# Seven block products in place of eight for w_out, and a written order of rounds, in a float32 FFT and MLP kernel

## The chip, the cores and the metric

The kernel runs on one core of one Trainium2 chip. The metric is the device time of one execution in microseconds. A core has engines that run side by side, each with its own queue of instructions: TensorE (PE; weight loads are shown apart as PEld), VectorE (DVE), ScalarE (ACT), GpSimd (POOL, not used here) and SyncE (SP), which issues the DMAs here. They wait for each other by semaphores. Matmuls write to PSUM (eight banks), from which ACT and DVE read.

## The reference

`x` is (8, 3008, 256) in float32; `w_in` is (256, 2048), `w_out` (2048, 256).

```python
X = np.fft.rfft(x, axis=1)
Xr, Xi = (X.real.astype(np.float32), X.imag.astype(np.float32))
Yr = Xr @ w_r - Xi @ w_i + b_r
Yi = Xr @ w_i + Xi @ w_r + b_i
lam = 0.01
Yr = np.sign(Yr) * np.maximum(np.abs(Yr) - lam, 0.0)
Yi = np.sign(Yi) * np.maximum(np.abs(Yi) - lam, 0.0)
Y = Yr.astype(np.float64) + 1j * Yi.astype(np.float64)
y = np.fft.irfft(Y, n=x.shape[1], axis=1)
...
h = np.maximum(x @ w_in, 0.0)
return (h * h @ w_out).astype(np.float32)
```

The second part takes `y`, as 24064 rows of 256.

## The kernel before

A transform of 3008 = 47 * 64 points is done as one of 47 and one of 64. Per batch: stage A (`fft_a`, 13 groups: load `xin`, fold to `f`, matmuls to `psa`, copy to `eva`, store to DRAM scratch), then for each of 12 pairs of residues (`fft_b`) stage B (load `bin`, matmuls to `psb`, copy to `x`), the mix with w_r and w_i (`psm1`, `psm2`, then bias and threshold in `e`, `t`, `z`) and stage C (`psc`, `evc`, store to a second scratch); at last stage D (`inverse`: load `din`, matmuls to `psd`, unfold to `dx`), which gives the columns `xt` of tokens for the two products with w_in and w_out.

Those two run over 52 chunks of columns: 48 of 470 tokens and 4 of 376. For each chunk and each of 16 blocks f of 128 hidden units, `moe_mm1` makes `ph` (L179 to L181), ReLU on ACT (L484) and a square on DVE (L485) give `g`, and `moe_mm2` adds the product with w_out to two PSUM accumulators `po`, one for each half of the 256 outputs. `moe_out` copies them out (L499) after the last f.

A float32 operand is split exactly into a high and a low part of 12 bits: `split` makes `gh` from `g` by a copy on ACT (L173) and `gl` by a subtraction on DVE (L174). `mm3` then uses three passes, high-high, high-low, low-high (L179, L180, L181), in a format called float32r. Some small products (B, D, and all of the first batch) take float32 operands whole; the trace then shows two instructions for one matmul.

The order is partly written and partly made by a scheduler. The main loop runs over chunks and f; `pend` and `LAG = 2` put the w_out product of an f two places behind its w_in product, and `active` is a list of generators (the transform of the next batch, stage D of the next chunk) from which each step takes as much as is due by a count of PE cycles. A tile framework then sets the final order on each engine by its own priorities, and places waits where a buffer or a value is not ready. Buffers come from pools: four PSUM banks for the transform (`ps_f`), two for `ph`, two for `po`. Ahead of the main loop stands the first batch with the weights: `load_win` and `load_wout` load pieces in turn, `narrow` makes float32 of 64-bit words (L217 to L222), and `split` cuts them.

Of the kernel before, what the change touches and what calls it, by code (L numbers as in the profile page):

```python
# [48 lines left out]
# Upper words of 2^-127 and of float32's largest value as float64, read as float32.  # L49
# [4 lines left out]
def groups_of(b):  # L54
    """The small group comes last in an even batch and first in an odd one, so that two meet."""
    return GROUPS if b % 2 == 0 else GROUPS[-1:] + GROUPS[:-1]


def token_order(b):
    """Position in the sequence of each column: by group of n2, n1 = 0..23, then n1 = 46..24."""  # L60
    n1 = np.r_[np.arange(NR), N1 - np.arange(1, NR)]
    return np.concatenate([((64 * n1[:, None] + 47 * (g + np.arange(w))) % S).reshape(-1) for g, w in groups_of(b)])


def folded_rows():
    """Positions in the sequence that are added and subtracted, by group: n1 and 47 - n1; -1 for none."""
# [10 lines left out]
def _cs(num, den):  # L77
    """cos and sin of 2 pi num / den, exact at the multiples of a quarter turn."""
# [8 lines left out]
def tables():  # L87
    """Transform matrices; they depend on the shapes alone."""
# [41 lines left out]

@with_exitstack
def fft_mix_moe(ctx: ExitStack, tc: tile.TileContext, xp, w_r, w_i, b_r, b_i,
# [5 lines left out]
    sb = ctx.enter_context(tc.tile_pool(name="sb", bufs=2))  # L138
    dr = ctx.enter_context(tc.tile_pool(name="dr", bufs=2, space=bass.MemoryType.DRAM))
    ps_f = ctx.enter_context(tc.tile_pool(name="ps_f", bufs=4, space=bass.MemoryType.PSUM))  # L140
    ps_h = ctx.enter_context(tc.tile_pool(name="ps_h", bufs=2, space=bass.MemoryType.PSUM))
    ps_o = ctx.enter_context(tc.tile_pool(name="ps_o", bufs=1, space=bass.MemoryType.PSUM))
# [14 lines left out]
    wmf = [sb.tile([P, 3, D], F32, tag="xh", name=f"wmf{k}", bufs=2) for k in range(2)]  # L157
# [4 lines left out]
    def ldt(name):  # L162
        return sb.tile([P, 512], F32, tag="ld", name=name, bufs=8)

    def evt(name):
        return sb.tile([P, 512], F32, tag="ev", name=name, bufs=4)

    def pst(name):
        return ps_f.tile([P, 512], F32, tag="f", name=name)

    def split(src, hi, lo):
        """src = hi + lo, exactly."""
# [3 lines left out]
    def mm3(out, lt, rt, start, stop):  # L176
# [79 lines left out]
    def rolling(pieces, depth):  # L256
        """Runs the pieces one per step, their loads `depth` steps ahead."""
        q = []
        for p in pieces:
            next(p)  # L260
            q.append(p)
            if len(q) > depth:
                for _ in q.pop(0):
                    pass
# [363 lines left out]
```

## Time and profile before

| | |
|---|---|
| median of 3 runs | 2694.76 us (2693.82 to 2699.69) |
| profiled execution, first to last instruction | 2694.1 us |
| mean granted TensorE clock | 0.996 |
| matmul records | 14088 |
| VectorE busy | 1841.4 us |
| ScalarE busy | 1434.1 us |
| first `ph` matmul begins at | 123.67 us |
| data moved by DMA | 163.44 MB |

In the profile a line of a group has the line of the program, engine, operation, output <- input, shape, count, then the busy time in us and the mean of one in ns, then the engine's idle time just ahead of them with what ended it. The chain of waits is followed back from the last instruction; each of its pieces has a start, a length, both in us, and its engine and line. A line of the stretches has the bounds in us, the length, the busy time and count of PE, PEld, DVE, ACT and POOL, then the granted clock, the share of the DMA engines and GB/s.

### The profile page before, as it was taken

To read this page: it belongs to the slowest core of one execution; us is meant where nothing else is said; L and a number is where in the kernel's file an instruction comes from. 1 tells how busy PE (TensorE), PEld (TensorE's weight loads), DVE (VectorE), ACT (ScalarE), POOL (GpSimd) and SP (SyncE) were. 2 spreads that over 40 slices of the span, in tenths; PEclk is the share of its full clock that TensorE was granted. 3 is DMA by queue.
4 is the path that set the end of the run, shared out by engine and by line. 5 is a ranking of instruction groups with operands and counts; after the bars stand their busy time and mean duration, and the time that the engine had idled before them with its cause. 6 is when DMAs were issued, how large, how long until landed. Compare 5 with 4: busy or idle time off the path is not lost.

```text
span 2694.1 us, 37380 instructions
## 1 busy us (share of the span) xinstructions
PE 2655.6 (99%) x14088; PEld 2387.3 (89%) x14088; DVE 1841.4 (68%) x3375; ACT 1434.1 (53%) x2649; POOL 0.2 (0%) x4
## 2 busy tenths in 40 slices
PE   6899999999999999999999999999999999999999
PEld 5689989989899898998989989899899989899888
DVE  5877766767667777667676776666767677655555
ACT  5755555545555555555555554555555555444444
POOL 0000000000000000000000000000000000000000
PEclk8999999999999999999999999999999999999999
DMA  8621122111221113211032110321103211100000
GB/s 239 203 69 50 45 87 75 45 40 35 79 89 43 45 34 97 75 39 49 27 97 70 46 52 21 107 68 42 49 20 107 70 43 34 47 31 21 8 15 15
DMA packets 113240, 163.44 MB, mean 61 GB/s; under 512 B 9267, under 2 KB 72995, under 8 KB 113059
## 3 DMA queue, kind: packets, MB, share of 16 engines
q1 hardware_dynamic: 113059, 161.05, 19.3%
q8 instruction: 111, 1.82, 0.3%
q14 instruction: 70, 0.57, 0.1%
HBM read 86.04 MB, written 74.97 MB: 60 GB/s over the span
## 4 chain that ended last, share of the span: by engine, by line
PE 95%; DMA 2%; DVE 1%; ACT 1%; issue 0%; SPq 0%; ACTq 0%; DVEq 0%
PE po L179 13%; PE ph L179 13%; PE po L180 13%; PE ph L180 13%; PE po L181 13%; PE ph L181 13%; PE psd L464 3%; PE psb L351 3%; PE psm L181 2%; PE psm L179 2%; PE psm L180 2%; PE psc L180 1%; PE psc L179 1%; PE psa L179 1%; PE psa L180 1%; PE psa L181 1%
## 5 line engine op out<-in xcount | busy, mean ns | idle before, releaser
L484 ACT ACTIVATE g<-ph 128x470 f32<-128x470 f32 (+1 forms) x832 | 463.0, 557 | 636.1 <-PE ph L181 633.1
L485 DVE TENSOR_TENSOR g<-g 128x470 f32<-128x470 f32 (+1 forms) x832 | 532.2, 640 | 355.1 <-ACT g L484 351.8
L174 DVE TENSOR_TENSOR gl<-g,gh 128x470 fp32r<-128x470 f32 (+1 forms) x832 | 532.2, 640 | 310.7 <-ACT gh L173 300.3
L173 ACT CAST gh<-g 128x470 fp32r<-128x470 f32 (+1 forms) x832 | 483.6, 581 | 416.4 <-DVE g L485 411.6
L179 PE MATMUL po<-gh,wo 128*128 128x470 f32 (+1 forms) x1664 | 644.7, 388 | 0.6
L179 PE MATMUL ph<-xt,wi 128*128 128x470 f32 (+1 forms) x1664 | 622.1, 374 | 1.2 <-ACT xt L173 1.2
L180 PE MATMUL po<-gl,wo 128*128 128x470 f32 (+1 forms) x1664 | 621.5, 374 | 0.0
L180 PE MATMUL ph<-xt,wi 128*128 128x470 f32 (+1 forms) x1664 | 620.4, 373 | 0.0
L181 PE MATMUL po<-gh,wo 128*128 128x470 f32 (+1 forms) x1664 | 619.9, 373 | 0.0
L181 PE MATMUL ph<-xt,wi 128*128 128x470 f32 (+1 forms) x1664 | 617.5, 371 | 0.0
L179 PEld LDWEIGHTS ph<-xt,wi 128*128 128x128 f32 x1664 | 314.3, 189 | 39.4 <-ACT xt L173 1.6
L181 PEld LDWEIGHTS po<-gh,wo 128*128 128x128 f32 x1664 | 314.0, 189 | 38.9
L180 PEld LDWEIGHTS ph<-xt,wi 128*128 128x128 f32 x1664 | 315.8, 190 | 36.4
L181 PEld LDWEIGHTS ph<-xt,wi 128*128 128x128 f32 x1664 | 313.1, 188 | 38.4
L179 PEld LDWEIGHTS po<-gh,wo 128*128 128x128 f32 x1664 | 314.7, 189 | 30.0 <-DVE o L499 2.9
L180 PEld LDWEIGHTS po<-gl,wo 128*128 128x128 f32 x1664 | 315.0, 189 | 26.1 <-DVE gl L174 0.6
L398 DVE TENSOR_TENSOR z<-e,t 64x256 f32<-64x256 f32 x336 | 140.9, 419 | 8.1
L179 PE MATMUL psm<-wm,xh 128*128 128x256 f32 x504 | 143.6, 285 | 0.0
L181 PE MATMUL psm<-wm,xl 128*128 128x256 f32 x504 | 142.3, 282 | 0.0
L180 PE MATMUL psm<-wm,xh 128*128 128x256 f32 x504 | 142.1, 282 | 0.0
L464 PE MATMUL psd<-tD,din 120*128 120x120 f32 (+1 forms) x832 | 126.4, 275 | 5.6 <-DMA din<-s 5.6
L351 PEld LDWEIGHTS psb<-tB,bin 128*128 128x128 f32 x768 | 109.4, 194 | 24.0 <-ACT tMs L173 13.6
(75 smaller groups left out, 2317.0 us busy)
## 6 DMA issues: line engine op xcount, KB each, us to landing
bin<-s SPq DMA_DIRECT2D x96, 256.0 KB
s<-evc SPq DMA_DIRECT2D x96, 256.0 KB
s<-eva SPq DMA_DIRECT2D x96, 240.0 KB
din<-s SPq DMA_DIRECT2D x96, 240.0 KB
outT_dram<-o SPq DMA_DIRECT2D x96, 235.0 KB
xin<-in_xp_dram SPq DMA_DIRECT2D x84, 240.0 KB
w<-in_moe_w_in_dram SPq DMA_DIRECT2D x8, 512.0 KB
w<-in_moe_w_out_dram SPq DMA_DIRECT2D x8, 512.0 KB
```

Of the source, the lines that this page charges most:

```text
L173: nc.scalar.copy(hi, src)
L174: nc.vector.tensor_sub(lo, src, hi.bitcast(F32))
L179: nc.tensor.matmul(out, l0, r0, start=start, stop=False)
L180: nc.tensor.matmul(out, l0, r1, start=False, stop=False)
L181: nc.tensor.matmul(out, l1, r0, start=False, stop=stop)
L351: nc.tensor.matmul(ps[:, k, :, q, :], tv[:, q, k], tB[:, 0:r + 2:r + 1], start=True, stop=True)
L398: nc.vector.tensor_sub(z[64 * c:64 * c + 64, q], e[src, c], t[src, c])
L464: nc.tensor.matmul(ps[:, k, part], t[:, s:s + P], tD[:n, tab + part, :n], start=True, stop=True)
L484: nc.scalar.activation(g[:, :n], ph[:, :n], AF.Relu)
L485: nc.vector.tensor_mul(g[:, :n], g[:, :n], g[:, :n])
```

## The change

It does three things.

**Seven products for eight.** Two blocks f, the two halves of the 256 outputs and two halves of a chunk's columns make a 2 x 2 by 2 x 2 block product, which is done with seven block products and some sums (a form of Strassen's scheme). The sums on the weights are made once, into `w7`, seven blocks of 128 x 128 for each pair of f, before the main part. The sums on the hidden values (`sums`) are made per pair on DVE, in `g`, now seven blocks of half the columns (236, with two columns shared by the halves; 188 in the short chunks). `split` is done on all seven at once (1652 columns). The square moves to ACT. The products stay in four PSUM banks (`PLACES`) and are put together after the last pair (`put_together`).

**Rounds written by hand.** The main part stands in `manual_schedule`, where the written order is each engine's order. A round r has the w_in product of pair r, the w_out product of pair r - 2, and at named places (`load`, a1, p1, v1, p2, a2, v2) the steps of the transform: `plan_a` (one group a round), `plan_b` (one pair of residues in three rounds), `plan_d` (two in a chunk of eight rounds). Stage B of a batch begins 51 rounds after that of the one before; A takes 13 of the rounds between.

**Buffers and the start.** The transform has two PSUM banks in place of four, `ph` has one buffer of two banks, `po` four banks. Everything of the first batch, all weights, and stage A of the second batch stand in `start`, in pools of their own, ahead of the rounds.

```diff
+PLACES = ((0, 0, 0), (2, 0, 1), (6, 1, 0), (5, 1, 1), (4, 2, 0), (3, 2, 1), (1, 3, 0))
+NPR = 7
+NU = NF // 2
+PAIR = 3
+TURN = 15
...
+                    def use(h, j=j):
+                        a = h.rearrange("p (f e m) -> p f e m", f=2, e=2)
+                        w7 = tl("w7", (P, NPR, P), bufs=1)
+                        nc.scalar.copy(w7[:, 0:3:2], a[:, :, 0])
+                        nc.scalar.copy(w7[:, 1], a[:, 1, 1])
+                        nc.vector.tensor_add(w7[:, 4], a[:, 0, 1], a[:, 1, 1])
+                        nc.vector.tensor_sub(w7[:, 6], w7[:, 4], a[:, 0, 0])
+                        nc.vector.tensor_sub(w7[:, 5], a[:, 0, 0], a[:, 0, 1])
+                        nc.vector.tensor_sub(w7[:, 3], a[:, 1, 0], w7[:, 6])
+                        split(w7, wo_[0][:, j], wo_[1][:, j])
...
+                r = r0 + i
+                at(r - 2, "load", load)
+                at(r, "v1", folded)
+                at(r, "a2", high)
+                at(r, "v2", low)
+                at(r + 1, "p1", points)
+                at(r + 1, "a2", out)
...
+                r = r0 + PAIR * i
+                at(r - 1 if i == 0 else r - 2, "load", load)
+                at(r, "p2", points)
+                at(r + 1, "a1", take)
...
+                at(r + 2, "p1", mix)
+                at(r + 2, "v2", biased)
+                at(r + 3, "v1", threshold)
+                at(r + 3, "a2", turned)
...
-        nc.scalar.activation(g[:, :n], ph[:, :n], AF.Relu)
-        nc.vector.tensor_mul(g[:, :n], g[:, :n], g[:, :n])
-        split(g[:, :n], gh[:, :n], gl[:, :n])
-        return gh, gl
+    def squares(c, ph):
+        m, t0 = halves(cols[c])
+        g = opnd("g", F32)
+        for t in range(2):
+            nc.scalar.activation(g[:, t:4:2, :m], ph[:, :, t * t0:t * t0 + m], AF.Relu)
+        nc.scalar.activation(g[:, 0:4, :m], g[:, 0:4, :m], AF.Square)
+        return g
+    def sums(c, g):
+        m, _ = halves(cols[c])
+        nc.vector.tensor_sub(g[:, 4:6, :m], g[:, 1:4:2, :m], g[:, 0:2, :m])
+        nc.vector.tensor_sub(g[:, 6, :m], g[:, 3, :m], g[:, 4, :m])
+        nc.vector.tensor_sub(g[:, 1, :m], g[:, 6, :m], g[:, 2, :m])
-    def moe_mm2(po, gg, n, f):
-        for k in range(2):
-            es = slice(k * P, k * P + P)
-            mm3(po[k][:, :n], (wo_[0][:, f, es], wo_[1][:, f, es]),
-                (gg[0][:, :n], gg[1][:, :n]), f == 0, f == NF - 1)
+    def mm2(c, j, po, gg):
+        m, _ = halves(cols[c])
+        for s, bank, half in PLACES:
+            mm3(po[bank][:, half * m:half * m + m], (wo_[0][:, j, s], wo_[1][:, j, s]),
+                (gg[0][:, s, :m], gg[1][:, s, :m]), j == 0 and half == 0, j == NU - 1,
+                skip_group_check=True)
...
+        nc.scalar.copy(p1, p[0])
+        add, sub = nc.vector.tensor_add, nc.vector.tensor_sub
+        add(o[0][:, 0], p[2], p1)
+        add(o[0][:, 1], p[6], p1)
+        add(o[1][:, 0], p[5], o[0][:, 1])
...
+    with tc.manual_schedule():
+        for r in range(last + LAG):
+            c, j = divmod(r, NU)
+            run(r, "load")
+            k = r - 1
+            if k in hid:
+                m, _ = halves(cols[k // NU])
+                gg[k] = opnd("gh", F32R), opnd("gl", F32R)
+                nc.scalar.copy(gg[k][0][:, :, :m], hid[k][:, :, :m])
+            run(r, "a1")
+            if r < last:
+                ph = mm1(c, j)
+            run(r, "p1")
+            if r < last:
+                g = squares(c, ph)
+            if k in hid:
+                nc.vector.tensor_sub(gg[k][1][:, :, :m], hid.pop(k)[:, :, :m],
+                                     gg[k][0][:, :, :m].bitcast(F32))
+            run(r, "v1")
+            if r < last:
+                sums(c, g)
+                hid[r] = g
+            k = r - LAG
+            if k >= 0:
...
+                mm2(cc, jj, pos[cc], gg.pop(k))
+            run(r, "p2")
+            run(r, "a2")
+            if k >= 0 and jj == NU - 1:
+                put_together(cc, pos.pop(cc))
+            run(r, "v2")
```

On PE, in the middle of the program, this stood for one f before (numbers in names tell buffers apart; two accumulators `po`):

```order
L179 MATMUL psm_12776<-wm_85,xh 128x256
L180 MATMUL psm_12776<-wm_86,xh 128x256
L181 MATMUL psm_12776<-wm_85,xl 128x256
L179 MATMUL po_12571<-gh,wo_909 128x470
L180 MATMUL po_12571<-gl,wo_909 128x470
L181 MATMUL po_12571<-gh,wo_910 128x470
L179 MATMUL po_12572<-gh,wo_909 128x470
L180 MATMUL po_12572<-gl,wo_909 128x470
L181 MATMUL po_12572<-gh,wo_910 128x470
```

After, the same lines of `mm3` are L186 to L188. This is the beginning of the w_out part of a round, with a product of stage C ahead of it:

```order
L186 MATMUL psc<-zh,tMs 128x512
L187 MATMUL psc<-zl,tMs 128x512
L188 MATMUL psc<-zh,tMs 128x512
L186 MATMUL po_12206<-gh,wo_529 128x236
L187 MATMUL po_12206<-gl,wo_529 128x236
L188 MATMUL po_12206<-gh,wo_530 128x236
L186 MATMUL po_12206<-gh,wo_529 128x236
L187 MATMUL po_12206<-gl,wo_529 128x236
L188 MATMUL po_12206<-gh,wo_530 128x236
L186 MATMUL po_12207<-gh,wo_529 128x236
```

Six matmuls of 470 columns for one f became 21 of 236 for two, in one stretch, and the transform's products stand at fixed places between the w_in and the w_out part.

On DVE, before, in the main part the square and the low part alternate for each f, with the transform's steps between them:

```order
L485 TENSOR_TENSOR g<-g 128x470
L357 TENSOR_TENSOR x<-x 128x256
L174 TENSOR_TENSOR gl<-g,gh 128x470
L174 TENSOR_TENSOR xl<-x,xh 128x768
L485 TENSOR_TENSOR g<-g 128x470
L174 TENSOR_TENSOR gl<-g,gh 128x470
L380 TENSOR_TENSOR e<-psm_11922,bias_82 128x512
```

After, two rounds of it (L801 is the low part of seven blocks, L750 to L752 are `sums`):

```order
L801 TENSOR_TENSOR gl<-g,gh 128x1652
L231 TENSOR_TENSOR x<-x 128x256
L697 TENSOR_TENSOR xt_9255<-dx,xt_9254 128x2x235
L750 TENSOR_TENSOR g<-g 128x472
L751 TENSOR_TENSOR g<-g 128x236
L752 TENSOR_TENSOR g<-g 128x236
L606 TENSOR_TENSOR xl<-x,xh 128x768
L801 TENSOR_TENSOR gl<-g,gh 128x1652
L639 TENSOR_TENSOR zl<-z,zh 128x512
L750 TENSOR_TENSOR g<-g 128x472
```

The low part of a round's pair stands between its sums and those of the next round, and every step of the transform (v1 ahead of the sums, v2 behind) has a fixed place in that cycle.

On DVE, around the begin of the main part, before: `wo` splits stand on both sides of the first squares (L485).

```order
L174 TENSOR_TENSOR xt_794<-dx,xt_793 128x2x235
L485 TENSOR_TENSOR g<-g 128x470 x2
L174 TENSOR_TENSOR gl<-g,gh 128x470
L218 TENSOR_SCALAR w_1059<-w_1059 128x512
L219 TENSOR_SCALAR w_1059<-w_1059 128x512
L174 TENSOR_TENSOR gl<-g,gh 128x470
```

After, this is one of eight pieces of w_out, all of them ahead of the first sums of hidden values (L319 and L320 narrow the next piece, L181 is the split):

```order
L324 SCALAR_TENSOR_TENSOR w_613<-w_614,w_613 128x512
L319 TENSOR_SCALAR w_655<-w_655 128x512
L364 TENSOR_TENSOR w_663<-w_613 128x128
L366 TENSOR_TENSOR w_663<-w_613 128x128
L365 TENSOR_TENSOR w_663<-w_663,w_613 128x128
L320 TENSOR_SCALAR w_655<-w_655 128x512
L367 TENSOR_TENSOR w_663<-w_613,w_663 128x128
```

Four pieces that were narrowed and split among the first products of the main part stand before it now, and each piece has four sums of 128 columns more.

More of the change, by code (lines that the diff above doesn't have):

```diff
@@ L160, in fft_mix_moe @@
     wo_ = []
[L162 to L169, printed above, removed]
     def split(src, hi, lo):
@@ L256, in rolling @@
[L256 to L264, printed above, removed]
-                yield
-        while q:
-            for _ in q.pop(0):
-                pass
-            yield
-    def ahead(n, load, depth):
-        got = [load(i) for i in range(min(depth, n))]
-        for i in range(n):
-            if i + depth < n:
-                got.append(load(i + depth))
-            yield i, got[i]
-            got[i] = None
@@ L590, in fft_mix_moe, with load_d, points_d @@
-    while pend:
-        do_mm2()
+        return [const.tile([P, 2, NCOL], F32R, tag=f"xt{k}", name=f"xt{k}", bufs=2) for k in range(2)]
+    def load_d(c, u, t):
+        b, g, w = chunks[c][u]
+        nc.sync.dma_start(out=t[:NR * w], in_=scr2[b][:, g:g + w, :])
+    def points_d(c, u, t, ps):
+        b, g, w = chunks[c][u]
+        n = NR * w
+        tab = 0 if w == W else 2
+        ps = ps[:, :4 * n].rearrange("p (k c m) -> p k c m", k=2, c=2)
+        for part in range(2):
+            for k in range(2):
+                s = part * D + k * P
+                nc.tensor.matmul(ps[:, k, part], t[:n, s:s + P], tD[:n, tab + part, :n],
+                                 start=True, stop=True)
+        return ps
@@ new lines, in plan_d, with load, points, take @@
+    def plan_d(c, u, r):
+        s = {}
+        def load():
+            if c not in xts:
+                xts[c] = alloc_x(c)
+            s["t"] = tl("din")
+            load_d(c, u, s["t"])
+        def points():
+            s["ps"] = points_d(c, u, s["t"], pst("psd"))
+        def take():
+            s["v"] = tl("xh", (P, 3, 2, P), name="dv").rearrange("p a b m -> p (a b m)")
+            s["v"] = s["v"][:, :2 * NR * W].rearrange("p (k m) -> p k m", k=2)
+            nc.scalar.copy(s["v"][:, :, :s["ps"].shape[3]], s["ps"][:, :, 1])
+        def unfolded():
+            s["x"] = tl("xl", (P, 3, 2, P), name="dx").rearrange("p a b m -> p (a b m)")
+            s["x"] = s["x"][:, :2 * N1 * W].rearrange("p (k m) -> p k m", k=2)
+            unfold(c, u, s["ps"], s["v"], s["x"])
+        def high():
+            m, (hi, lo) = part_x(c, u, xts[c])
+            nc.scalar.copy(hi, s["x"][:, :, :m])
+        def low():
+            m, (hi, lo) = part_x(c, u, xts[c])
+            nc.vector.tensor_sub(lo, s["x"][:, :, :m], hi.bitcast(F32))
+        at(r - 2, "load", load)
+        at(r, "p1", points)
+        at(r, "a2", take)
+        at(r, "v2", unfolded)
+        at(r + 1, "a1", high)
+        at(r + 1, "v1", low)
@@ new lines, in fft_mix_moe, with pair_round @@
+    first = [next(c for c, ch in enumerate(chunks) if any(u[0] == b for u in ch)) for b in range(B)]
+    stage_b = {1: 2}
+    for b in range(2, B):
+        stage_b[b] = stage_b[b - 1] + PAIR * NPAIR + TURN
+    done = {b: r + PAIR * (NPAIR - 1) + 9 for b, r in stage_b.items()}
+    def pair_round(r):
+        return all((r - r0) % PAIR == 0 for r0 in stage_b.values() if r0 <= r < r0 + PAIR * NPAIR)
+    for b, r in stage_b.items():
+        if b > 1:
+            plan_a(b, r - TURN)
+        plan_b(b, r)
@@ new lines, in fft_mix_moe, with mm1 @@
+    for c in range(1, nch):
+        rounds = [r for r in range(NU * (c - 1) + 1, NU * c - 1) if pair_round(r)]
+        for u in (1, 0):
+            r = rounds.pop()
+            assert r - 2 >= done.get(chunks[c][u][0], 0) - 2 and r >= 2, (c, u, r)
+            plan_d(c, u, r)
+    def mm1(c, j):
+        n = cols[c]
+        ph = ps_h.tile([P, 2, 512], F32, tag="h", name="ph")
+        for a in range(2):
+            f = 2 * j + a
+            fs = slice(f * P, f * P + P)
+            for k in range(2):
+                mm3(ph[:, a, :n], (wi_[0][:, k, fs], wi_[1][:, k, fs]),
+                    (xts[c][0][:, k, :n], xts[c][1][:, k, :n]), k == 0, k == 1)
+        return ph
```

716 lines of the change are left out of this document (380 added, 336 removed).

## Prediction

> **What bounds the kernel now.** I read the page's busy table first, then the chain that ended last, then the stretches, then groups kept apart by shape.
>
> ```profile
> PE 2655.6 (99%) x14088; PEld 2387.3 (89%) x14088; DVE 1841.4 (68%) x3375; ACT 1434.1 (53%) x2649; POOL 0.2 (0%) x4
> PE 95%; DMA 2%; DVE 1%; ACT 1%; issue 0%; SPq 0%; ACTq 0%; DVEq 0%
> 100.00:110.00 10.00, 8.37 (x33) 5.28 (x31) 8.96 (x24) 7.48 (x15) 0.00 (x0) 1.00 0.83 250
> 110.00:120.00 10.00, 4.44 (x19) 4.21 (x19) 6.30 (x14) 4.25 (x8) 0.00 (x0) 0.76 0.76 243
> 200.00:700.00 500.00, 499.91 (x2733) 454.24 (x2732) 359.14 (x669) 267.69 (x498) 0.00 (x0) 1.00 0.17 53
> 2200.00:2600.00 400.00, 399.88 (x2054) 360.24 (x2053) 245.92 (x430) 198.04 (x366) 0.00 (x0) 1.00 0.09 28
> ```
>
> PE carries 95% of the chain, and in the two long stretches it is busy all the time at full clock, while VectorE (DVE) is at 72% and 61%, ScalarE (ACT) at 54% and 50%. So from the first `ph` product to the last `po` product every matmul costs its spacing. Busy shares can't price a matmul, since records overlap; spacings are read from the chain, where each piece ends at the next start.
>
> ```profile
> 999.70 0.12 PE psm L179
> 999.81 0.12 PE psm L180
> 999.93 0.12 PE psm L181
> 1000.41 0.44 PE psd L464 x4
> 1000.85 0.22 PE po L179
> ...
> 1003.42 0.12 PE psm L179
> ```
>
> ```profile
> 1044.21 0.42 PE psd L464 x4
> ```
>
> The twelve 470-column products from 1000.85 to 1003.42 take 2.57, 0.214 us each; those with 256 moving columns take 0.119 (three rows). Four products with 120 moving columns (whole float32) take 0.44, and four with 96 take 0.42: 0.110 and 0.105 each. A fifth fewer columns and hardly less time: these are not bound by what streams. They share a stationary tile of 128 columns, so I read 0.105 to 0.110 as the floor that loading it sets.
>
> ```profile
> L180 PE MATMUL po<-gl,wo 128*128 128x470 f32 x1536 | 578.9, 377 | 0.0
> L180 PE MATMUL po<-gl,wo 128*128 128x376 f32 x128 | 42.7, 333 | 0.0
> L180 PEld LDWEIGHTS po<-gl,wo 128*128 128x128 f32 x1664 | 315.0, 189 | 26.1 <-DVE gl L174 0.6
> L180 PEld LDWEIGHTS psa<-fl,tAs 96*96 96x96 f32 x12 | 2.0, 163 | 0.3
> ```
>
> A record of 376 columns is 44 ns shorter than one of 470, hence 0.170 apart. Thirty-two stationary columns cost 26 ns of load, so 128 cost 104: the same floor from the load's side.
>
> **The products with w_out.** Before, three passes of 1536 + 128 records each: 4608 x 0.214 + 384 x 0.170 = 1051 us. After, a pair of f takes 21 products (7 blocks, 3 passes) of half the columns in place of 12: in 48 chunks 48 x 8 x 21 = 8064 of 236 columns, in the four short chunks 672 of 188. No record here has so few columns with these operands. Streaming: from 256 to 470 the spacing grows (0.214 - 0.119) / 214 = 0.44 ns a column, so 236 columns give 0.110. Floor: 0.105 to 0.110. Both meet at one value; I take 0.111 for 236 and 0.110 for 188: 895 + 74 = 969 us, **82 us less**. Bounds: 0.105 (48 us less than taken) and the 256-column 0.119 (65 us more).
>
> The Trainium skill, "TensorE: Matmul & The Clock Gate", section "Back-to-back issue gap", prices one isolated product at N/2.4 + 2.5 ns: an estimate of 101 ns for 236 columns, 81 ns for 188, with which the products come to 868 us and the total falls 101 us below mine. The row of 256 columns stands at 119 where that gives 109, so the trace doesn't follow it here. In the other direction, "Perfetto Trace Analysis", section "Identifying the Most-Contended Engine", judges PE by the summed time of the weight loads; 3744 more loads of 189 ns speak against this change, and as an exclusive cost they would add 708 us. The 256-column rows, 119 ns apart with loads of 189, show loads that overlap. What is here of the pages enters no term of the sum.
>
> Every other product (w_in, and A, B, mix, C, D of later batches) keeps count and shape.
>
> **What moves ahead of the main part.** All eight w_out pieces are now split, as seven blocks, before the first `ph`. Before, half stood there already.
>
> ```profile
> L220 DVE SCALAR_TENSOR_TENSOR w<-w,w 128x512 uint32<-128x512 uint32 x12 | 8.2, 685 | 0.1
> L222 DVE SCALAR_TENSOR_TENSOR w<-w,w 128x512 uint32<-128x512 uint32 x12 | 8.2, 683 | 0.0
> L218 DVE TENSOR_SCALAR w<-w 128x512 f32<-128x512 f32 x12 | 5.1, 422 | 2.8 <-ACT w L217 2.8
> L174 DVE TENSOR_TENSOR wo<-w,wo 128x512 fp32r<-128x512 f32 x4 | 2.8, 690 | 1.7 <-ACT wo L173 1.7
> L174 DVE TENSOR_TENSOR tMs<-tM,tMs 128x128 fp32r<-128x128 f32 x1 | 0.3, 286 | 0.0
> 50.00:60.00 10.00, 8.97 (x45) 6.72 (x44) 8.57 (x16) 8.35 (x18) 0.00 (x0) 1.00 0.71 200
> ```
>
> Twelve narrowed pieces are eight of w_in and four of w_out. DVE gets four more pieces at 2 x 0.42 + 0.69 + 0.68 + 0.69 = 2.9 (11.6 us), eight times four sums of 128 columns at about 0.29 (9.3), and eight splits of 896 instead of 512 columns, 0.40 more each at about 1.04 ns a column (3.2): 24 us. In the six stretches from 50 to 110 us (the first and the last are quoted) DVE is busy 81 to 95%, so little idle time hides this; I take **25 us**, within 10 (gaps swallow a part) and 35 (ACT's 13 us more for the same pieces don't overlap). What follows the last store of C stays:
>
> ```profile
> 106.41 5.55 DMA s<-evc
> 111.97 3.50 DMA din<-s
> 123.67 0.69 PE ph L179 x2
> ```
>
> So the first `ph` moves from 123.7 to about 149.
>
> **Filling and draining.** An item now spans two f. Round 0 has no `po` work to cover its ReLU, and `gh` stands ahead of the next ReLU on ACT: so PE waits about 1.1 us for the first ReLUs and 2.6 for the second. At the end it waits for the last `gl`: ReLUs to `gl` take 7.0 by the durations below, the two w_out parts before it 4.7, so 2.4; and seven sums of 236 columns (about 0.40 each, first row below) and one copy replace one copy of 0.65: 2.4 more. Together **9 us**.
>
> **Does PE still set the pace?** Rows for the new vector work:
>
> ```profile
> L470 DVE TENSOR_TENSOR dx<-psd,dv 128x240 f32<-128x240 f32 x96 | 38.6, 402 | 1.9 <-ACT dv L469 1.9
> L485 DVE TENSOR_TENSOR g<-g 128x470 f32<-128x470 f32 x768 | 497.0, 647 | 330.1 <-ACT g L484 327.0
> L174 DVE TENSOR_TENSOR xl<-x,xh 128x768 fp32r<-128x768 f32 x84 | 80.4, 957 | 10.1 <-ACT xh L173 7.0
> L484 ACT ACTIVATE g<-ph 128x470 f32<-128x470 f32 x768 | 432.0, 563 | 600.2 <-PE ph L181 598.0 <-ACT xt L173 0.2
> L173 ACT CAST gh<-g 128x470 fp32r<-128x470 f32 x768 | 451.1, 587 | 381.3 <-DVE g L485 377.3
> L173 ACT CAST xh<-x 128x768 fp32r<-128x768 f32 x84 | 70.1, 835 | 1.7 <-DVE x L357 0.5
> L311 DVE TENSOR_TENSOR f<-xin 120x256 f32<-120x256 f32 x84 | 35.3, 421 | 11.2 <-DMA xin<-in_xp_dram 10.4
> ```
>
> By their slopes (1.04 ns a column on DVE, 0.83 on ACT) a round has on DVE sums of 0.65 + 0.40 + 0.40 and `gl` of 1652 columns at 1.88; on ACT two ReLUs at 0.56, a square of 944 at 0.98, `gh` at 1.57. The written order closes two rings. DVE: sums, `gh`, `gl`, the v1 steps, next sums: 4.90 + v1. ACT: ReLUs, square, sums, `gh`, the a1 steps, next ReLUs: 5.12 + a1. PE's round is 12 x 0.214 + 21 x 0.111 = 4.90 plus transform products.
>
> - Rounds with B, mix, C (the rest of 416, about 273): 8 x 0.110 + 18 x 0.119 + 3 x 0.233 (512 columns, by 0.44 ns a column) over three rounds, and 0.22 for D, make 6.36 on PE; the rings reach about 6.1. PE leads.
> - Rounds with A (78): 6 x 0.119 + 0.22 make 5.83; DVE's ring with the fold (0.84), D's split and its share of the output sums is 5.9 to 6.2. Short 0.1 to 0.37.
> - Rounds with D alone (the last 65): PE 5.12, rings 5.2 to 5.4. Short 0.1 to 0.28.
>
> ```profile
> 1001.28 0.41 DVE L470 TENSOR_TENSOR dx<-psd,dv 128x240 f32<-128x240 f32 x1
> 1001.60 0.39 DVE L471 TENSOR_TENSOR dx<-psd,dv 128x230 f32<-128x230 f32 x1
> ```
>
> The lower ends allow for an instruction starting 0.09 before the record ahead of it ends, as the second of these does. That is 15 us at the lower ends, 47 at the upper, and 0 if two rounds of lead absorb it. I take **15**: independent neighbours, where the overlap holds, are most. PE's products wait for `gl` of two rounds before, PSUM for evacuations a round old, and `bin` and `din` are fetched one to two rounds (6 to 12 us) ahead, against 3.5 us for `din` above: no term. The four output banks are freed in the order in which the next chunk's products open them, a w_in product (2.57) later: no term; without that cover up to 2.8 us a chunk.
>
> **Sum.** 2694.1 (the profiled span, within 0.7 us of the 2694.76 median) - 82 + 25 + 9 + 15 = **2661 us**.
>
> **Rivals.**
> - *A half-width product costs as much as one of 256 columns.* Price 0.119, place: every `po` product. For it: load and stream meet at this size, and the spacing may settle above both. Against: the 96 to 120-column rows lie at 0.105 to 0.110. It decides from 0.115 on (32 us over 8064 products); at 0.119 the time is 2661 + 65 = **2726**, slower.
> - *The rings set the pace.* Each dependent step takes its full record: 47 for 15, 2693; unchanged. Against it stand rounds with B where PE has 0.25 to spare.
> - *The start costs little and the rings nothing.* 2661 - 15 - 15 = 2631. For it: DVE's idle tenth before 110 us.
> - *No floor and no fixed part:* 236/470 of 0.214 is 0.107, 32 us less: 2629. For it: the 96-column row already lies under that. Against: 256 columns at 0.119 are above their share, 0.117. The isolated-gap rule of the page above would go further down this way.
> - *Loads count in full:* 3744 x 0.189, about 3370; the 256-column rows speak against it.
> - *It doesn't do what it says:* the built order shows 21 products a pair, so hardly; about 2694.
>
> **How the numbers follow.** Forecast (2640 to 2685) 0.50; half-width price 0.20; rings 0.13; cheap start 0.10; no floor 0.04; full loads 0.02; not as it says 0.01. Of the rings' case 0.05 still ends faster. Faster by over 0.2% (about what a measurement of this kernel can tell from no change): 0.50 + 0.10 + 0.04 + 0.05 = 0.69; within 0.2%: 0.08 + 0.01 = 0.09; slower: 0.20 + 0.02 = 0.22. The range runs from the cheap start (2628) to most of the half-width case (2718).
>
> **What would show it.** Chain pieces of `po` at 0.11 (right) or 0.12 (the rival); 14088 - 4992 + 8736 = 17832 products; the first `ph` near 149; in rounds with B no PE gaps, in rounds with A and in the last 65 gaps of 0.1 to 0.4 a round released by DVE's `gl` or ACT's ReLU. PE gaps in B rounds, or a `po` spacing over 0.115, would make it wrong.

## The result, and the profile after

| | before | after |
|---|---|---|
| median | 2695.1 us (2693.82 to 2699.69) | 2755.26 us (2751.99 to 2757.75) |
| ratio | | 1.022, 95% interval 1.0205 to 1.0234 |
| profiled span | 2694.1 us | 2756.0 us |
| first `ph` matmul | 123.7 us | 164.4 us |
| first `ph` to the end | 2570.5 us | 2591.6 us |
| PE's own work in that part | 2562.1 us | 2487.6 us |
| PE's stalls in that part | 8.4 us | 104.0 us |

The change costs 60 us, where 33 less were forecast. The last two rows are worked out from the starts of all matmuls: each shape has a spacing when nothing is waited for (0.2139 us for 470 columns, 0.1119 for 236, 0.1185 for 256, 0.111 for 120 or fewer); count times spacing is PE's own work, and the rest of the time is stall. So the 61.9 us between the two spans are 40.7 (start) - 74.5 (products) + 95.6 (stalls). One price doesn't hold everywhere: the 1512 products of the mix (`psm`, 256 columns) start 0.114 us apart as a median in this kernel, 0.119 before. So PE's own work is up to 7 us too large here and the stalls as much too small; the same holds for e1 to e3, e6 and e14 below.

The busy table and the chain of waits of the kernel after:

```profile
PE 2621.9 (95%) x17832; PEld 2443.3 (89%) x17832; DVE 2160.0 (78%) x3383; ACT 2050.9 (74%) x2917; POOL 0.2 (0%) x4
PE 65%; DVE 15%; ACT 14%; issue 3%; DMA 3%; SPq 0%; ACTq 0%; DVEq 0%
```

PE has as many matmuls as forecast (17832), but its share of the chain fell from 95% to 65%; DVE and ACT have 29% of it in place of 2%. The same two stretches as before (span, then busy time of PE, PEld, DVE, ACT, POOL; PE's clock last but two):

```profile
200.00:700.00 500.00, 487.89 (x3412) 460.72 (x3411) 404.62 (x626) 386.10 (x553) 0.00 (x0) 0.99 0.18 54
2200.00:2600.00 400.00, 394.18 (x2705) 369.25 (x2704) 306.02 (x454) 291.02 (x394) 0.00 (x0) 1.00 0.11 33
```

PE idles 12 us of 500 and 6 of 400, where it idled 0.1 before. No other engine is full: DVE has 81% and 77%. So as a mean nothing lacks throughput, and what is late may be late by its place in a queue; e12 below bears that out. Two groups by shape, and the chain in one product with w_out (the first two and the last of 21 pieces):

```profile
L801 DVE TENSOR_TENSOR gl<-g,gh 128x1652 fp32r<-128x1652 f32 x384 | 721.4, 1879 | 355.0 <-ACT gh L793 355.0
L793 ACT CAST gh<-g 128x1652 fp32r<-128x1652 f32 x384 | 604.3, 1574 | 399.0 <-DVE g L752 217.0 <-PE po L188 117.3 <-DVE e L237 53.2
```

```profile
1012.62 0.12 PE po L186
1012.74 0.12 PE po L187
...
1014.87 0.11 PE po L188
```

The new vector work costs what was forecast (`gl` 1.88, `gh` 1.57), and so does the half-width product: the 21 pieces begin between 1012.62 and 1014.87, 2.25 / 20 = 0.112 us apart.

**Where PE stalls.** Call a round what lies from the first `ph` product of a pair to that of the next. Over the 415 rounds that have a next one the stalls are 94.3 us, and 64 of them lie in 52 rounds: the round after each chunk's last product. One of them, on DVE and then on PE (start, duration, in brackets the idle time ahead and what ended it):

```profile
279.37 0.40 DVE L770 TENSOR_TENSOR o<-po,p 128x236 f32<-128x236 f32 x1 [0.98 <-ACT p L768]
...
281.57 0.39 DVE L776 TENSOR_TENSOR o<-o,po 128x236 f32<-128x236 f32 x1
281.87 0.40 DVE L268 TENSOR_TENSOR dx<-psd,dv 128x240 f32<-128x240 f32 x1
282.31 0.40 DVE L269 TENSOR_TENSOR dx<-psd,dv 128x230 f32<-128x230 f32 x1
```

```profile
282.85 0.47 PE L186 MATMUL psc<-zh,tMs 128*128 128x512 f32 x1 [1.40 <-DVE dx L269]
```

The seven output sums take 2.5 us, from 279.37 to 281.87. Behind them in DVE's queue stand the two steps (L268, L269) that read `psd`. `psc` needs a bank of the two that the transform's products share, and gets it when L269 has read `psd`; so PE waits 1.40 us. More often it is no bank but an operand of the next round that stands behind the same sums: `fl` (L557) in rounds with A, which `psa` reads, and `xl` (L606), which the mix reads. In all of the kernel (who waited <- for what: us, times, longest):

```profile
PE psa L187 <- DVE fl L557: 17.2, 13, 2.6
PE psm L188 <- DVE xl L606: 15.4, 13, 2.1
PE psc L186 <- DVE dx L269: 10.9, 8, 1.5
```

Of these, 16.3, 14.4 and 10.9 us lie in the 52 rounds after a chunk's last product.

**The start.** Stretches of 10 us, same columns; before the change DVE had 8.96, 6.30 and 5.86 in the first three of these four, and `ph` began at 123.7:

```profile
100.00:110.00 10.00, 9.90 (x41) 7.82 (x42) 9.98 (x25) 9.04 (x19) 0.00 (x0) 0.80 0.49 136
110.00:120.00 10.00, 4.41 (x11) 2.65 (x10) 9.76 (x23) 8.23 (x18) 0.00 (x0) 0.72 0.33 111
120.00:130.00 10.00, 6.38 (x19) 3.50 (x18) 9.48 (x23) 8.04 (x16) 0.00 (x0) 0.84 0.21 67
130.00:140.00 10.00, 3.78 (x6) 1.79 (x6) 0.00 (x0) 1.85 (x4) 0.00 (x0) 0.50 0.51 144
```

Until 130 DVE is full. Then it idles for 10 us, and `ph` is still 34 us away. The chain of waits there:

```profile
130.15 2.08 PE psc L456 x2
...
136.43 5.38 DMA xin<-in_xp_dram
...
142.39 3.78 PE psa L409 x8
...
146.85 4.52 DMA s<-eva
...
152.92 4.45 DMA xin<-in_xp_dram
...
157.96 5.74 PE psa L409 x16
...
164.38 3.38 DMA s<-eva
...
168.13 1.03 ACT g L743 x2
```

`xin`, `psa` and `eva` belong to stage A of batch 1: its loads come one after another, and even the first ReLU (168.13) waits for its last store. (The start has pools of its own; that the ReLU waits because it writes to memory that the store still reads is argued from that, not shown.)

### The profile page after: what moved, and what is told of

Same layout as the page of the kernel before. It is cut to its first block, busy times and chain, and to the rows that moved or that the text cites. A ratio compares the mean times of both kernels' runs of the same rounds, so it can differ in the third digit from the quotient of the medians.

```text
span 2756.0 us, 45108 instructions
## 1 busy us (share of the span) xinstructions
PE 2621.9 (95%) x17832; PEld 2443.3 (89%) x17832; DVE 2160.0 (78%) x3383; ACT 2050.9 (74%) x2917; POOL 0.2 (0%) x4
## 4 chain that ended last, share of the span: by engine, by line
PE 65%; DVE 15%; ACT 14%; issue 3%; DMA 3%; SPq 0%; ACTq 0%; DVEq 0%
PE ph L186 9%; PE ph L187 9%; PE ph L188 8%; PE po L188 8%; PE po L187 8%; PE po L186 8%; ACT gh L793 6%; DVE gl L801 3%; PE psd L261 2%; PE psb L223 2%; ACT g L743 2%; DVE g L750 2%; ACT g L744 2%; PE psm L188 2%; PE psm L186 2%
## 5 line engine op out<-in xcount | busy, mean ns | idle before, releaser
L801 DVE TENSOR_TENSOR gl<-g,gh 128x1652 fp32r<-128x1652 f32 (+1 forms) x416 | 770.4, 1852 | 384.1 <-ACT gh L793 384.1
L793 ACT CAST gh<-g 128x1652 fp32r<-128x1652 f32 (+1 forms) x416 | 645.7, 1552 | 438.7 <-DVE g L752 241.8
L186 PE MATMUL po<-gh,wo 128*128 128x236 f32 (+1 forms) x2912 | 811.6, 279 | 2.2 <-DVE o L775 1.4
L187 PE MATMUL po<-gl,wo 128*128 128x236 f32 (+1 forms) x2912 | 803.8, 276 | 2.4 <-DVE gl L801 2.4
L188 PE MATMUL po<-gh,wo 128*128 128x236 f32 (+1 forms) x2912 | 805.0, 276 | 0.0
L186 PE MATMUL ph<-xt,wi 128*128 128x470 f32 (+1 forms) x1664 | 634.0, 381 | 6.1 <-ACT g L743 5.3
L188 PE MATMUL ph<-xt,wi 128*128 128x470 f32 (+1 forms) x1664 | 619.0, 372 | 0.0
L186 PEld LDWEIGHTS po<-gh,wo 128*128 128x128 f32 x2912 | 559.9, 192 | 10.3 <-DVE o L775 2.7
L187 PEld LDWEIGHTS po<-gl,wo 128*128 128x128 f32 x2912 | 559.5, 192 | 7.7 <-DVE gl L801 2.8
L188 PEld LDWEIGHTS po<-gh,wo 128*128 128x128 f32 x2912 | 561.3, 193 | 0.0
L743 ACT ACTIVATE g<-ph 128x472 f32<-128x472 f32 (+1 forms) x832 | 417.4, 554 | 105.0 <-PE ph L188 100.3
L744 ACT ACTIVATE g<-g 128x944 f32<-128x944 f32 (+1 forms) x416 | 408.8, 983 | 13.2
L186 PEld LDWEIGHTS ph<-xt,wi 128*128 128x128 f32 x1664 | 316.1, 190 | 40.0 <-ACT g L743 8.6
L188 PEld LDWEIGHTS ph<-xt,wi 128*128 128x128 f32 x1664 | 314.5, 189 | 39.0
L750 DVE TENSOR_TENSOR g<-g 128x472 f32<-128x472 f32 (+1 forms) x416 | 266.7, 641 | 41.5 <-ACT g L744 28.0
L752 DVE TENSOR_TENSOR g<-g 128x236 f32<-128x236 f32 (+1 forms) x416 | 166.5, 400 | 14.4
L751 DVE TENSOR_TENSOR g<-g 128x236 f32<-128x236 f32 (+1 forms) x416 | 166.5, 400 | 14.3
L188 PE MATMUL psm<-wm,xl 128*128 128x256 f32 x504 | 142.2, 282 | 15.4 <-DVE xl L606 15.4
L186 PE MATMUL psm<-wm,xh 128*128 128x256 f32 x504 | 140.0, 278 | 0.0
```

Source lines behind the costliest of these rows:

```text
L186: nc.tensor.matmul(out, l0, r0, start=start, stop=False, **kw)
L187: nc.tensor.matmul(out, l0, r1, start=False, stop=False, **kw)
L188: nc.tensor.matmul(out, l1, r0, start=False, stop=stop, **kw)
L743: nc.scalar.activation(g[:, t:4:2, :m], ph[:, :, t * t0:t * t0 + m], AF.Relu)
L744: nc.scalar.activation(g[:, 0:4, :m], g[:, 0:4, :m], AF.Square)
L750: nc.vector.tensor_sub(g[:, 4:6, :m], g[:, 1:4:2, :m], g[:, 0:2, :m])
```

## The experiments

"Start" is the first `ph`; "stalls" are those of the 415 rounds, in us. The kernel before took 2694.6 to 2695.4 us as a median beside these runs.

| run | what differs | time, us | ratio to before (95%) | start | stalls |
|---|---|---|---|---|---|
| after | | 2755.26 | 1.0205 to 1.0234 | 164.4 | 94.3 |
| e1 | v2 steps ahead of output sums | 2719.31 | 1.0072 to 1.0102 | 165.6 | 55.9 |
| e2 | loads of stage A ahead | 2747.29 | 1.0177 to 1.0207 | 155.8 | 91.2 |
| e3 | e1 and e2 | 2711.61 | 1.0043 to 1.0073 | 158.3 | 53.7 |
| e4 | after, but eight full-width products | 2730.0 | 1.0112 to 1.0146 | 155.7 | 5.7 |
| e5 | e3, `gh` and `gl` later, three rounds of lag | 3032.75 | 1.1234 to 1.1268 | 158.6 | 376.8 |
| e6 | after, half of the w_out pieces | 2741.46 | 1.0157 to 1.0187 | 149.6 | 94.3 |
| e7 | e5, w_out sums on GpSimd | 3025.78 | 1.1209 to 1.1243 | 154.7 | 376.5 |
| e8 | e5, inverse of chunk 0 ahead | 3035.27 | 1.1236 to 1.1274 | 158.5 | 379.3 |
| e9 | e5, three buffers for the squares | 2719.98 | 1.0076 to 1.0104 | 158.7 | 67.4 |
| e10 | e9, w_out sums on GpSimd | 2717.08 | 1.0066 to 1.0094 | 154.8 | 67.2 |
| e11 | e9, output sums ahead of `gl` | 2687.66 | 0.9960 to 0.9981 | 159.3 | 32.6 |
| e12 | e11, w_out sums on GpSimd | 2680.89 | 0.9941 to 0.9968 | 153.1 | 31.9 |
| e13 | e12, both `din` loads of chunk 0 together, its inverse ahead | 2687.35 | 0.9955 to 0.9980 | 156.0 | 38.6 |
| e14 | after, inverse of chunk 0 ahead | 2755.47 | 1.0205 to 1.0233 | 164.7 | 92.1 |
| e15 | e3, v1 steps behind the sums | 3100.04 | 1.1474 to 1.1509 | 159.6 | 446.8 |

**e1, e2, e3: the two suspects by themselves.** In e1 the output sums go to the end of DVE's round:

```diff
             run(r, "p2")
             run(r, "a2")
+            run(r, "v2")
             if k >= 0 and jj == NU - 1:
                 put_together(cc, pos.pop(cc))
-            run(r, "v2")
```

> One edit: at the end of a chunk the v2 steps of the transform stand ahead of the seven output sums on VectorE, not behind them. Theory A (PE stalls after each chunk because the step its next transform product needs, or that frees its PSUM bank, is queued behind the output sums): the round after a chunk end, now 1.23 us too long on average over 52 chunks (64 us), falls under 0.3; time 2690 to 2705. Theory B (the sums, gh, gl cycle is too long whatever the order): the same excess is spread elsewhere, time 2745 to 2757.

e2 gives the loads of stage A of batch 1 six buffers of their own and issues six of them ahead; e3 has both.

> One edit: in the start, the loads of stage A of the second batch have six buffers of their own and are issued six units ahead. Theory A (the late loads, seen as pieces of 5.4 and 4.5 us in the chain before the first ph, make most of the start's extra time): the first ph falls from 164.4 to 148 to 153, time 2738 to 2745. Theory B (VectorE's added weight work sets it): first ph 160 or later, time 2750 or more.

> The edits of v2 first and of the start together. If both causes are right and independent the gains add: 2675 to 2692, faster than before the change. If the stalls only move: over 2700.

e1 took 36 us off, and the round after a chunk's end fell from a mean stall of 1.23 us to 0.11 (52 rounds). e2 took 8, with the start 8.6 earlier. Together they took 43.7, so they are two causes. Both fell short of their numbers, and e3 missed its range by 20. Part of the stalls only moved: 58 us left the round after a chunk's end, and 20 came back in others, 11.5 of them in the round behind it (a mean of 0.33 us for 0.11), where `fl`, `xl` and `dx` now come late. What else was left (with these, 0.31 us in each round with A, 0.25 in plain ones) had been counted as small.

**e4: the written order with eight products.** From the kernel after, with its order of steps (v2 last in the round): `ph` to `g` in one ReLU, the square on DVE, four blocks of w_out in place of seven, two copies of `po`, one of them on DVE, in place of the sums.

```diff
-        for s, bank, half in PLACES:
...
-            mm3(po[bank][:, half * m:half * m + m], (wo_[0][:, j, s], wo_[1][:, j, s]),
...
+        for a in range(2):
+            for k in range(2):
+                mm3(po[k][:, :n], (wo_[0][:, j, 2 * a + k], wo_[1][:, j, 2 * a + k]),
...
```

> The written rounds alone: eight full-width products (12 matmuls of 470 columns a pair of f), square on VectorE, two copies out at a chunk's end; no w7 sums. Theory A (half-width products cost 0.112 us and save 82 us; the loss is the output sums at chunk ends and the start): PE's own work in the main part rises by about 80 us, the excess over it falls from 94 to 10 to 30 us, first ph about 158, time 2755 to 2775. Theory B (the rounds themselves, with two transform banks and fixed places, cause the stalls): excess stays at 70 or more, time over 2815.

The same two stretches in e4:

```profile
200.00:700.00 500.00, 499.80 (x2731) 454.36 (x2730) 311.31 (x412) 266.01 (x399) 0.00 (x0) 1.00 0.18 54
2200.00:2600.00 400.00, 400.00 (x2061) 361.03 (x2061) 217.19 (x257) 183.97 (x249) 0.00 (x0) 1.00 0.09 30
```

With 311 in place of 405 us of DVE in the first of them, the same cycle of rounds has no stalls (5.7 in all). From first `ph` to the end e4 takes 2571.2 us, the kernel before 2570.5. So the written order by itself costs nothing there; the stalls come with the seven products. Two things come with them that e4 doesn't part: more vector work, and rounds that are 0.18 us shorter on PE (74 us over 416 rounds). In the rounds as written they eat the gain: 74 us less on PE, 89 more stalls (94.3 - 5.7), and 38 of those go with the place of the seven output sums (e1), which e4 doesn't have. e4 came out 25 us under its range: its stalls fell below the 10 us allowed for, and its start came 8.7 us earlier than in the kernel after.

**e6 and e14: the start.** e6 prepares pieces 0 to 3 of w_out alone (`wo_[0][:, j % 4, s]` in the products), so half of w_out is left out of the computation. e14 loads both `din` of chunk 0 at once and writes the inverse ahead of what is left of stage A of batch 1.

> The changed kernel, but only four of the eight w_out pieces are loaded, narrowed, summed and split; the products of pairs 4 to 7 read the blocks of pairs 0 to 3, so half of w_out is left out of the computation. The count of products stays. If DVE's work on the pieces is what makes the start later, four pieces are worth 4 x (2.9 narrowing + 1.16 sums + 1.09 split) = 20.6 us: first ph 164.4 -> about 144, time 2755 -> 2734. If the loads from DRAM set it (2 MB less of them): about 8 us. If the start is late by the order of stages alone: under 5 us.

> The changed kernel with that edit of the start alone. Its first ph came 40.7 us later than before: 28 until the last psc (131.2 against 103.1) and 12.6 from there to the first ph (33.2 against 20.6). If the rest of stage A of batch 1, whose loads and products stand ahead of the inverse, is the second part, the first ph comes 8 to 13 us earlier, 152 to 156, and the time falls from 2755 to 2743 to 2748. If stage A is then wanted at once by rounds 0 to 2, the gain is given back there and the time stays.

e6: the start comes 14.8 us earlier, between its first two cases. So the work on four pieces counts; how much of it is DVE's, ACT's or the loads', which all go with a piece, e6 doesn't part (e7 below moves a part of DVE's alone). e14: the last `psc` ends about where it did (131.0 for 132.2 in the kernel after), `psd` comes at 138.5 in place of 150.9, and yet `ph` begins at 164.7. Its chain of waits:

```profile
128.94 2.08 PE psc L456 x2
...
138.47 3.75 PE psd L261 x16
142.25 3.35 DMA xin<-in_xp_dram
...
146.44 4.51 DMA xin<-in_xp_dram
...
155.10 4.44 DMA xin<-in_xp_dram
...
164.66 0.76 PE ph L186
```

The inverse isn't what the main part waits for: stage A of batch 1 ends last in either order, by loads that follow each other through four buffers. Six loads ahead (e2) bring 8.6 us; another order (e14, e8) brings nothing.

**e5, e7, e8: cut the rings, and close another.** In e5 `gh` and `gl` stand at the end of a round and the product with w_out lies three rounds behind:

```diff
-    LAG = 2
+    LAG = 3
...
             run(r, "v1")
             if r < last:
                 sums(c, g)
-                hid[r] = g
+            run(r, "a2")
+            run(r, "v2")
...
                 mm2(cc, jj, pos[cc], gg.pop(k))
+            p = r - 1
+            if p in hid:
...
+                nc.scalar.copy(gg[p][0][:, :, :m], hid[p][:, :, :m])
+                nc.vector.tensor_sub(gg[p][1][:, :, :m], hid.pop(p)[:, :, :m],
+                                     gg[p][0][:, :, :m].bitcast(F32))
```

> From the kernel with both edits (2711.6 us), the two rings are cut: on ACT a2 and then gh stand behind the square, on DVE the sums and v2 stand ahead of gl, and the product with w_out lies three rounds behind in place of two. Same work on every engine; a ring no longer holds sums, gh, gl and the next sums in one round. If the rings make the 54 us of stalls that are left in the main part (0.31 a round with A, 0.25 in plain rounds), the stalls fall under 20 us and the time to 2672 to 2682 (one round more of filling costs 0 to 5). Rival, the two PSUM banks that the transform's products share (psd waiting 8.7 us for evc): the stalls stay at 40 or more, time 2700 to 2712. Rival, an engine's own work (DVE 78% busy as a mean): stalls stay in rounds with A (0.3 each), go in plain rounds: about 2692.

> As the run with the rings cut, and the four sums of each w_out piece (32 of 128 columns, 284 ns each on DVE, 9.1 us in all) go to GpSimd. If DVE's work sets the start, the first ph comes about 9 us earlier than in that run and the time falls by 9. If the latency of the chain through zh, psc and the scratch sets it, or GpSimd's own pace, nothing to 3 us, or later.

> As the run with the rings cut, and in the start the inverse transform of chunk 0 is written ahead of all that is left of stage A of batch 1, which before stood between its first load and its products. If those matmuls (5.4 + 4.7 us in the chain at half clock) and the stores that SyncE has queued ahead of the din load hold the first ph, it comes 8 to 14 us earlier and the time falls by 6 to 14, less what stage A then takes in rounds 0 and 1. If the order of the start is set by other waits, under 3 us.

All of e5's cases failed: 3032.75 us. The largest waits of e5 (who waited <- for what: us, times, longest):

```profile
ACT g L756 <- DVE gl L824: 656.7, 361, 3.1
DVE g L763 <- ACT g L757: 545.0, 365, 7.4
```

`g` has two buffers, so a ReLU takes the one that `gl` of the round before reads last. With `gl` at the end of DVE's round this closes a longer ring: ReLUs 1.02, square 0.99, sums 1.45, v2 steps, `gl` 1.88, next ReLUs: 5.34 and v2, against 5.00 of PE's work in a plain round, which took 5.87. e7 against e5 prices the sums of w_out on DVE: the start 3.9 us earlier, the time 7.0 less, between its two cases (9, and nothing to 3). e8 agrees with e5 in time and start, so the order of the start alone is worth nothing there.

**e9, e10: a third buffer.** The squares get a tile with three buffers; the three sums one of their own with two, to save room; so `gh` and `gl` are made in two instructions each.

```diff
-        g = opnd("g", F32)
+        g = tl("g", (P, 4, HALF), bufs=3), tl("gs", (P, 3, HALF), bufs=2)
```

> The run with the rings cut had closed another: with gl at the end of DVE's round and two buffers of g, the next but one ReLU waited for gl (656.7 us in 361 waits). Here the four squares get three buffers and the three sums a tile of their own with two, so that ReLU waits for gl of a round earlier; gh and gl are made in two instructions each (0.1 to 0.2 us more a round on ACT and on DVE), and the copy of po goes into an output tile. If the rings were the 54 us of stalls left with both edits, stalls fall under 20 us and the time to 2670 to 2685. Rival, PSUM banks and evacuations of the transform: stalls of 40 or more, 2700 to 2715. If a third thing shares the blame (DVE's own work in rounds with A), stalls stay in rounds with A alone, 0.2 to 0.3 each: 2690.

> As the run with the third buffer, and the four sums of each w_out piece go to GpSimd. That took 4 us from the first ph and 7 from the time in the pair of runs with the rings cut, half of DVE's 9.1: here 4 to 7 us less again, 2664 to 2680 by the ring theory. The version meant to beat both kernels.

Of e5's 377 us of stalls 309 are gone, but none of e9's cases came true: at 2720 us it is 8 slower than e3. e10, with the sums of w_out on GpSimd, took 3 off and missed its range too. What is left changed its place: 41 of e9's 67 us lie in the round after a chunk's end, 0.79 each. In e9, there, on DVE and on PE:

```profile
2554.28 0.89 DVE L827 TENSOR_TENSOR gl<-gs,gh 128x708 fp32r<-128x708 f32 x1
2555.09 0.40 DVE L784 TENSOR_TENSOR o<-po,o 128x236 f32<-128x236 f32 x1
```

```profile
2555.54 0.38 PE L186 MATMUL po<-gh,wo 128*128 128x236 f32 x1 [0.95 <-DVE o L784]
```

The next chunk's first `po` product waits for an output sum to free its bank, since the sums stand behind `gl`, which ended at 2555.17. In the other rounds the stalls are 26 us, where e3 had 48 outside the round after a chunk's end.

**e11, e12, e13: output sums ahead of `gl`.** `gl` is wanted two rounds later, so the sums can pass it:

```diff
+            if k >= 0 and jj == NU - 1:
+                put_together(cc, pos.pop(cc))
             p = r - 1
             if p in hid:
```

> In the run with the third buffer the stalls of 67 us were in one place: the round after a chunk's last product, 0.79 us as a mean of 52 (41 in all, po waiting for the output sums), while the other rounds ran at PE's own work, A included. There the seven output sums stood behind gl. Here they stand ahead of gh and gl (gl is wanted two rounds later). If this order is what is left, stalls fall by 30 to 41 us, time 2679 to 2690, and it beats the kernel before. If the sums only push gh and gl into the next round's ReLU or sums, the stalls come back in the second or third round after the chunk's end: 2700 or more.

> As the run with the output sums ahead of gl, and the four sums of each w_out piece go to GpSimd: 3 to 7 us less, 2674 to 2686.

> From the best version so far (2680.9 us; first ph 153.1, last psc 127.6, psd products from 137.7 to 147.3): both din loads of chunk 0 are issued together and ahead of what is left of stage A of batch 1. In the kernel before the psd products lay 3.3 us apart, first to last, here 9.6. If the second load, issued behind the products of the first and behind the stores of stage A, holds the first ph, it comes about 6 us earlier and the time is 2673 to 2677. If PE or the order of stage A holds it, under 2 us.

e12, busy table, chain and the two stretches:

```profile
PE 2602.3 (97%) x17832; PEld 2437.1 (91%) x17832; DVE 2173.4 (81%) x3767; ACT 2083.7 (78%) x3333; POOL 17.0 (1%) x36
PE 88%; DVE 5%; ACT 4%; DMA 2%; issue 1%; POOL 0%; SPq 0%; DVEq 0%; ACTq 0%; POOLq 0%
200.00:700.00 500.00, 499.42 (x3505) 472.45 (x3504) 418.69 (x721) 403.75 (x654) 0.00 (x0) 1.00 0.19 55
2200.00:2600.00 400.00, 399.86 (x2768) 378.49 (x2767) 310.44 (x529) 306.00 (x465) 0.00 (x0) 1.00 0.10 28
```

With more vector work than after (DVE 419 us in the first stretch for 405), PE is busy all the time again. e11 is faster than the kernel before (0.997), and e12 by 14 us (0.9955, 0.9941 to 0.9968). e13 was no gain: the two `psd` groups came together, and stage A of batch 1 ended last all the same; its time is 6 us over e12, of which 3 are the start.

**e15: which of the two rings.** From e3, the v1 steps behind the sums:

```diff
-            run(r, "v1")
             if r < last:
                 sums(c, g)
                 hid[r] = g
+            run(r, "v1")
```

> From the kernel with both edits (2711.6 us, stalls 53.7: A 0.31, plain 0.25 a round), one move: on DVE the v1 steps stand behind the sums of g in place of ahead of them, which takes them out of DVE's ring (4.90 + v1 becomes 4.90) and leaves ACT's ring (5.12 + a1) as it is. If DVE's ring is the one that holds, stalls fall by 10 to 20 us: 2692 to 2702. If ACT's ring holds, under 5 us. The fold of stage A and the later fl come 1.45 us later too: if the transform's own steps are short of time, rounds with A get worse.

Neither of the first two, and far beyond the third: 388 us slower than e3, in rounds of every kind. On DVE, then on ACT:

```profile
2601.88 0.65 DVE L763 TENSOR_TENSOR g<-g 128x472 f32<-128x472 f32 x1 [0.93 <-ACT g L757]
...
2603.78 0.69 DVE L635 TENSOR_TENSOR e<-e,t 128x512 f32<-128x512 f32 x1
```

```profile
2604.50 0.41 ACT L643 COPY z<-e 64x256 f32<-64x256 f32 x1 [2.66 <-DVE e L635]
...
2606.77 1.57 ACT L806 CAST gh<-g 128x1652 fp32r<-128x1652 f32 x1
```

The threshold (L635, a v1 step) now ends after the sums, 2.66 us later than ACT could turn `e` to `z`. ACT's `gh` stands behind those copies, `gl` waits for `gh`, and the next sums stand behind `gl`: one ring through both engines. This is a round with B; such rounds have some 284 of the 447 us, and what held the others was not followed. So the question that the run was for, whether DVE's or ACT's ring held in e3, stays open. What it shows is the price of a place: the same instructions with the same durations, 14% of the time.

## Why the prediction was wrong

It forecast 2661; 2755 was measured, with the other sign. By its terms (profiled spans):

| term | predicted | measured |
|---|---|---|
| products with w_out | -82 | -74 |
| first `ph` later | +25 | +40.7 |
| filling and draining | +9 | about +10 |
| "... PSUM for evacuations a round old ...: no term" | 0 | 38 (e1), and 8 more |
| rings | +15 | not shown apart: some 39 are left, of which e11 has 21 less than e3 |

Filling is 4.9 us in rounds 0 and 1, draining 5.5 more than before; with 38, 8 and 39 that makes the 95.6 us of stalls.

**Products: right, a little mis-sized.** The price was 0.1119 us, not 0.111: 8064 x 0.0009 = 7 us. The rival of the 256-column price is out. The Trainium skill, "TensorE: Matmul & The Clock Gate", section "Back-to-back issue gap", gives 101 ns for 236 columns as an isolated gap (its formula; an estimate), and warns there that the isolated gap under-counts short products in a stream, which these 112 ns agree with. The Trainium skill's other rule, to judge PE by the summed time of the weight loads ("Perfetto Trace Analysis", section "Identifying the Most-Contended Engine"; it names PE's share of its peak rate beside it), would not have told the three kernels apart: PEld stands at 89%, 89% and 91% of the span before, after and in e12.

**The failing step is the list behind "no term": "PE's products wait for `gl` of two rounds before, PSUM for evacuations a round old".** The list left out the transform's own low parts `fl` and `xl`, which PE reads in the very next round, and it took the banks to be freed a round ahead, where `psc` and `psd` share two and one comes free by a step of the same round. `fl`, `xl` and that step are v2 steps of DVE. They were queued behind seven output sums, 2.5 us once a chunk. The prediction priced these sums in DVE's share and at the end of the kernel, but never asked what stands behind them, though the written order showed it. In the 52 rounds concerned PE waited 30.7 us for the two operands and 10.9 for the bank. e1 changed that order alone: 38 us of stalls and 36 us of time. The sign "PE gaps in B rounds" came true there too: rounds with B have 34 us of stalls in this place. Another 8 us (7.5 in four waits; 6.8 in e12) are rounds in which A, C and D all want a bank and `psd` waits for the copy `evc`.

**Rings: the means came out as forecast, the mechanism isn't shown.** Once e1 was in (e3), rounds with A stalled by 0.31 us each and plain ones by 0.25 (0.19 without rounds 0 and 1), B rounds hardly (0.04), which lies in the forecast ranges. But a ring that is too long costs round after round, and these stalls stand in a few. Number a chunk's rounds from 0, the one of its first w_in product. Of the 78 rounds with A, the 29 at places 3, 5 and 6 have 22 us, the other 49 together under 4; of the last 65, the 16 at places 0 and 2 have 9.7 us, the other 49 under 4. Nor does PE wait there for `gl` or the ReLU, as the forecast's sign had it, but for these (e3):

```profile
PE psd L261 <- ACT evc L661: 8.1, 4, 2.3
PE psa L187 <- DVE fl L570: 4.9, 9, 0.9
PE ph L187 <- DVE xt L710: 3.6, 7, 0.6
```

So that the means fit is luck, as far as the runs show. A tight ring may still leave DVE no time to catch up behind a rare step, and no run parts that; e5 and e15 show that a longer ring does set the pace. The reason given for the lower ends, "independent neighbours, where the overlap holds, are most", doesn't hold for the steps of a ring: `gl` waited 355 us in all for ACT's `gh`. e11 has 21 us less than e3, and the last 65 rounds fell from 13.5 us to 0.7; its edits (later `gh` and `gl`, the third round of lag, the third buffer, the place of the output sums) were not told apart. Of the 32 us that remain in e12, 4 are filling and 7 the waits for `evc`; the rest was not told apart either.

**Start: DVE's term held, "what follows the last store of C stays" did not.** The last `psc` begins at 131.2 for 103.1 before, 28 later for a term of 25, and e6 (119.3) and e7 (128.6, against 133.2 in e5) show that work on the pieces moves it. From there to `ph` it is 33.2 us for 20.6: 12.6 that the forecast didn't have. Stage A of batch 1 now ends last, by its loads; the chain before had no `xin` there. e2 gets back 8.6.

**Right:** 17832 products, overlapping loads, the durations of all new vector work, PE's lead in B rounds away from chunk ends. The gain was real: with the order changed it is 14 us in e12, not 33. By the spans of the profiled executions e12 has -74 (products) + 29 (start) + 29 (stalls) = -16, for the forecast's -82 + 25 + 24.

## What to carry to other kernels

Work taken from the bounding engine and given to others is paid for in their queues: do not only sum each engine's time in a round, but follow from each thing that the bounding engine needs next (operand or free bank) back through every instruction queued ahead of its maker. A rare long step, here 2.5 us in eight rounds, belongs behind all that the next round needs, and ahead of what is wanted two rounds later. A loop over two engines can be cut by a buffer and a round of lag, but count the buffers on every tile of the loop: one short (e5), and the new loop is longer than the old.

## What the runs showed of the hardware

- A half-width product needs 0.112 us, though the record of its weight load is longer than that; so the loads of neighbours overlap each other, not only the products. One pass of it in the kernel after, by shape:

```profile
L187 PEld LDWEIGHTS po<-gl,wo 128*128 128x128 f32 x2912 | 559.5, 192 | 7.7 <-DVE gl L801 2.8
```

- The same product can have two spacings: those of the mix start 0.119 us apart before and 0.120 in e9 to e13, but 0.114 in the kernel after and in e1 to e3 (medians over 1100 to 1400 pairs of starts behind 200 us). Why is open.
- Where PE had little to do in the start, its granted clock was low: 0.50 in the stretch from 130 to 140 us of the kernel after, where PE was busy for 3.78 us, and 0.58 in the next. Products of `psa` began 0.426 us apart there, against 0.216 in the first 60 us. So the products behind such a wait ran slower, too.
- Sums of 128 columns took 513 to 584 ns on GpSimd (e12) and 284 on DVE. The Trainium skill, "GPSIMD Engine Reference", section "Engine selection", states that GpSimd is about twice as slow as VectorE for elementwise operations of two inputs, and this trace agrees (1.8 to 2.1 times). They were worth moving all the same, 3 to 7 us, since GpSimd was idle and DVE was not.
